# ScalarE computes the exact square of the hidden chunk in 26 slots, and adds the small term to the softmax sums

## The chip, the cores and the metric

The kernel runs on one core of a Trainium2 chip. The core has a matrix engine (TensorE, in the profile PE, with its weight loads as PEld), a vector engine (VectorE, DVE), an activation engine (ScalarE, ACT), a general engine (GpSimd, POOL) and a queue engine that issues most transfers (SyncE, SP). Each engine runs its own instruction list in order; semaphores hold an instruction until what it needs is done. The metric is the device time in microseconds of one execution, lower is better.

## The reference

Windowed attention, then a dense feed-forward layer with a squared ReLU, then eight experts of which each token uses one.

```python
scores = scale * np.matmul(q, k.transpose(0, 1, 3, 2))      # 4 x 8 heads, 576 positions, 64 wide
mask = (rel >= 0) & (rel < window)                          # window = 64
attn = np.exp(scores - np.max(scores, axis=-1, keepdims=True))
attn = attn / (np.sum(attn, axis=-1, keepdims=True) + 1e-09)
x = attn @ v                                                # 2304 tokens x 512
...
h = np.maximum(x @ w_in, 0.0)                               # w_in 512 x 2048
x = h * h @ w_out                                           # w_out 2048 x 512
...
expert_idx = np.argmax(x @ w_gate, axis=1)                  # 8 experts
out[mask] = gate_w[mask, None] * (np.maximum(xe @ w1[e], 0.0) @ w2[e])
```

## The kernel before

**Split numbers.** Products keep nearly full precision by splitting each operand into a rounded high part and a low part (the rest). `mm3` (lines 171 to 174) then makes three products: high by high, high by low, low by high.

**The dense layer in chunk slots.** Tokens go in 9 super-tiles of 256 (`st`), the 2048 hidden columns in 16 chunks of 128 (`f`). A slot is one pair (st, f): `gemm1` makes the chunk's 128 x 256 hidden values in a PSUM bank `h` (12 matmuls of 256 columns), `hidden` takes the ReLU into `r` on ScalarE (L462), `square` and `square_low` make the square as a high part `gh` and a low part `gl`, and two slots later `gemm2` adds the chunk to the output banks `y` (6 matmuls of 512 columns). There are two `h` banks, so `gemm1` of a slot waits until `gl` of the slot two before has been made. Slots 0 to 31 take super-tiles 0 and 1 in turns; the other 112 follow one super-tile after the other.

**The square before.** ScalarE squares `r` and rounds it in one instruction (L469, `gh`). VectorE makes the exact square `max(h, 0) * r` from the bank and `r` and writes it to the other half of the bank (L471), and then subtracts `gh` from it (L478, `gl`).

**Weight conversion.** In the first part of the dense layer the weights arrive as 64-bit numbers and are turned into fp32 on the chip, 16 conversions (0 to 15), one for each chunk f: a transfer to a staging tile, an absolute value on ScalarE (`conv_a`, L189), four VectorE instructions on 128 x 1024 words (`conv_b`, L205, L206, L207, L210), then two roundings on ScalarE and two subtractions (`conv_c`, L226 and L228) that stand mostly on GpSimd, every sixth on VectorE. Staging and work tiles (`stg`, `tmp`) hold two conversions; the transfer for conversion f + 2 is issued when conversion f's last VectorE instruction is done.

**Attention beside it.** For each of 36 groups: scores on TensorE, for later groups a mask and a maximum on VectorE (L383, L387), four exponentials with row sums on ScalarE, then `att_norm`: VectorE adds 1e-9 to the sums (L410) and inverts them (L411), GpSimd multiplies (L412). GpSimd also lays out the queries (L334).

**Order.** The code names the slot at which each piece is written, but up to the last dense super-tile the final order on each engine is chosen by a scheduler at build time; the expert part after that is written out by hand.

Of the kernel before, what the change touches and what calls it, by code (L numbers as in the profile page):

```python
# [16 lines left out]
ACTF = mybir.ActivationFunctionType  # L17
ALU = mybir.AluOpType
# [31 lines left out]
def kernel(  # L50
# [13 lines left out]
    nc = tc.nc  # L64
# [6 lines left out]
    NF = DFF // P  # L71
    ST = 256
# [50 lines left out]
    for half in range(2):  # L123
# [5 lines left out]
            out=mid, in_=mid, pattern=[[-1, P]], compare_op=ALU.is_ge, fill=NEG, base=W, channel_multiplier=1  # L129
# [260 lines left out]
    def att_exp(g):  # L390
        s, nmax = probs[g]
        tot = br.tile([P, HP], F32, "tot", 3)
        if g < NE:
            ps, s = s, sfirst[g % 4]
            for hp in range(HP):
                nc.scalar.activation(
                    s[:, hp, :], ps[:, hp * P:(hp + 1) * P], ACTF.Exp, bias=nmax[:, hp:hp + 1], scale=SCALE,
                    accum_out=tot[:, hp:hp + 1],
                )
            probs[g] = s, tot  # L400
            return
        for hp in range(HP):
            nc.scalar.activation(
                s[:, hp, :], s[:, hp, :], ACTF.Exp, bias=nmax[:, hp:hp + 1], accum_out=tot[:, hp:hp + 1]
            )
        probs[g] = s, tot

    def att_norm(g):
        s, tot = probs[g]
        nc.vector.tensor_scalar_add(tot, tot, 1.0e-9)  # L410
        nc.vector.reciprocal(tot, tot)  # L411
        nc.gpsimd.tensor_tensor(s, s, tot.unsqueeze(2).to_broadcast([P, HP, P]), op=ALU.mult)  # L412

# [51 lines left out]
    def square(st, f):  # L465
        ps, r = gT[st, f]
        gh = br.tile([P, ST], F32R, "gh", 3)
        gl = br.tile([P, ST], F32R, "gl", 3)
        nc.scalar.square(gh, r)  # L469

        nc.vector.scalar_tensor_tensor(  # L471
            out=ps[:, ST:2 * ST], in0=ps[:, :ST], scalar=0.0, in1=r, op0=ALU.max, op1=ALU.mult
        )
        gT[st, f] = ps, gh, gl

    def square_low(st, f):
# [403 lines left out]
    slot = {c: i for i, c in enumerate(order)}  # L880
# [12 lines left out]
    def chain(i, stages, x, gaps, most=2):  # L893
# [8 lines left out]
        return i  # L902

    ATT = (att_scores, att_max, att_exp, att_norm, att_transpose, att_evac, att_values, att_out)
    at(16, load_gates, 0)

# [18 lines left out]
    for g in range(2 * QB, NS * QB):  # L925
        st, j = divmod(g, QB)
# [19 lines left out]
    for i in range(-PRE, len(order) + LA):  # L946
        run(i, False)
        if 0 <= i - 1 < len(order):
            square(*order[i - 1])
            square_low(*order[i - 1])  # L950
        if 0 <= i < len(order):
            gemm1(*order[i])
        if i >= LA:
            st, f = order[i - LA]
            gemm2(st, f)
            if f == NF - 1:
                x2_out(st)
        run(i, True)
        if 0 <= i < len(order):
            hidden(*order[i])  # L960
# [194 lines left out]
```

## Time and profile before

| | |
|---|---|
| median of 3 runs | 835.53 us (834.1 to 836.63) |
| profiled execution | 832.06 us, of which its span 829.9 us |
| TensorE busy | 787.3 us, 95% of the span |
| VectorE busy | 530.4 us, 64% |
| ScalarE busy | 398.8 us, 48% |
| GpSimd busy | 269.9 us, 33% |
| mean granted TensorE clock | 0.987 |

The span runs from the first to the last instruction. Shares are means over stages with different limits: the conversion lies between about 10 and 131 us, the dense layer between about 34 and 522 us, the experts after it.

### The profile page before, as it was taken

How to read it: one execution, taken by the hardware profiler on the slowest of the kernel's cores; microseconds unless marked ns; L12 is line 12 of the kernel's file. 1: busy time of each engine (PE TensorE's matmuls, PEld its weight loads, DVE VectorE, ACT ScalarE, POOL GpSimd, SP SyncE). 2: the span in 40 equal slices, each digit the busy share in tenths (PEclk: the TensorE clock that was granted, in tenths of full speed). 3: DMA queues.
4: the chain of work that ended last, by engine and by line, in shares of the span. 5: the costliest groups of instructions: out<-in, count | busy, mean ns of one | idle time of the engine just before them, and what ended most of it. 6: DMA issues, size and time to landing. Idle time of an engine off the chain costs nothing.

```text
span 829.9 us, 14957 instructions
## 1 busy us (share of the span) xinstructions
PE 787.3 (95%) x5212; PEld 685.5 (83%) x5212; DVE 530.4 (64%) x1198; ACT 398.8 (48%) x1051; POOL 269.9 (33%) x262
## 2 busy tenths in 40 slices
PE   6889989999999999999999999989999999999894
PEld 5777878888888888888888897877898888888783
DVE  5799995984855947639467396568678654434110
ACT  6986663434444443534344345447577553434211
POOL 4646751112121221312211016165567541420201
PEclk9989999999999999999999999999999999999998
DMA  9845553111111111102020037366678644420101
GB/s 264 274 134 190 194 172 102 64 34 32 58 45 64 39 42 62 52 29 75 26 64 18 22 102 229 104 216 208 193 244 246 212 155 131 135 80 2 51 2 43
DMA packets 50860, 91.50 MB, mean 110 GB/s; under 512 B 8220, under 2 KB 24604, under 8 KB 50752
## 3 DMA queue, kind: packets, MB, share of 16 engines
q1 hardware_dynamic: 44688, 80.43, 30.3%
q0 software_dynamic: 6064, 9.63, 3.5%
q8 instruction: 69, 1.13, 0.6%
q14 instruction: 39, 0.32, 0.1%
HBM read 84.59 MB, written 13.81 MB: 119 GB/s over the span
## 4 chain that ended last, share of the span: by engine, by line
PE 66%; issue 13%; DVE 9%; DMA 5%; ACT 4%; POOL 1%; ACTq 0%; SPq 0%; POOLq 0%; DVEq 0%
PE h L172 11%; PE h L173 10%; PE h L174 10%; PE y L172 10%; PE y L174 9%; PE y L173 9%; PE a L360 2%; DMA stg<-in_moe_w_out 2%; PE a L433 2%; PE a L418 1%; DVE tmp L205 1%; DVE tmp L210 1%; PE a L683 1%; DVE tmp L207 1%; DMA out<-s,tab 1%
## 5 line engine op out<-in xcount | busy, mean ns | idle before, releaser
L172 PE MATMUL h<-xh,w 128*128 128x256 f32 (+3 forms) x864 | 262.9, 304 | 10.9 <-DVE gl L478 5.4
L174 PE MATMUL h<-xh,w 128*128 128x256 f32 (+3 forms) x864 | 255.6, 296 | 1.2 <-POOL w L228 1.2
L173 PE MATMUL h<-xl,w 128*128 128x256 f32 (+3 forms) x864 | 255.6, 296 | 0.9 <-DVE xl L169 0.5
L172 PEld LDWEIGHTS h<-xh,w 128*128 128x128 f32 x864 | 164.9, 191 | 27.6 <-DVE gl L478 9.6
L173 PEld LDWEIGHTS h<-xl,w 128*128 128x128 f32 x864 | 165.0, 191 | 9.1 <-DVE xl L169 0.9
L174 PEld LDWEIGHTS h<-xh,w 128*128 128x128 f32 x864 | 165.0, 191 | 4.3 <-POOL w L228 1.5
L462 ACT ACTIVATE r<-h 128x256 f32<-128x256 f32 x144 | 55.1, 382 | 203.7 <-PE h L174 197.9
L172 PE MATMUL y<-w,gh 128*128 128x512 f32 x294 | 119.2, 405 | 0.7 <-ACT gh L469 0.7
L770 DVE SCALAR_TENSOR_TENSOR ggl<-h,ggh 128x512 fp32r<-128x512 f32 (+1 forms) x69 | 46.2, 670 | 111.6 <-ACT ggh L769 111.5
L173 PE MATMUL y<-w,gh 128*128 128x512 f32 x294 | 116.4, 396 | 0.0
L471 DVE SCALAR_TENSOR_TENSOR h<-h,r 128x256 f32<-128x256 f32 x144 | 61.4, 426 | 84.0 <-ACT r L462 84.0
L174 PE MATMUL y<-w,gl 128*128 128x512 f32 x294 | 102.1, 395 | 0.5 <-DVE gl L770 0.5
L769 ACT ACTIVATE ggh<-h 128x512 fp32r<-128x512 f32 (+1 forms) x69 | 40.2, 583 | 125.5 <-PE h L174 96.2
L548 DVE SCALAR_TENSOR_TENSOR tmp<-tmp,stg 128x512 f32<-128x512 f32 x128 | 96.0, 750 | 0.8
L334 POOL COPY q<-qd 64x256 f32<-64x256 f32 x46 | 34.4, 749 | 143.9 <-PE a L360 142.5
L172 PE MATMUL y<-w,ggh 128*128 128x512 f32 x170 | 70.7, 416 | 0.0
L174 PE MATMUL y<-w,ggl 128*128 128x512 f32 x170 | 67.6, 398 | 1.7 <-DVE junk L996 1.1
L173 PE MATMUL y<-w,ggh 128*128 128x512 f32 x170 | 67.1, 395 | 0.0
L276 POOL TENSOR_TENSOR w<-stg,w 128x512 fp32r<-128x512 f32 x27 | 36.5, 1357 | 90.6 <-ACT w L275 87.6
L478 DVE TENSOR_TENSOR gl<-h,gh 128x256 fp32r<-128x256 f32 x144 | 60.5, 420 | 8.3 <-ACT gh L469 1.5
L172 PEld LDWEIGHTS y<-w,gh 128*128 128x128 f32 x294 | 55.6, 189 | 10.8 <-ACT gh L469 1.4
L173 PEld LDWEIGHTS y<-w,gh 128*128 128x128 f32 x294 | 55.6, 189 | 9.4
(165 smaller groups left out, 1262.4 us busy)
## 6 DMA issues: line engine op xcount, KB each, us to landing
stg<-in_moe_w SPq DMA_DIRECT2D x45, 512.0 KB, 4.0
stgx<-in_moe_w SPq DMA_DIRECT2D x18, 512.0 KB, 4.2
stg<-in_moe_w_in SPq DMA_DIRECT2D x16, 512.0 KB, 4.0
stg<-in_moe_w_out SPq DMA_DIRECT2D x16, 512.0 KB, 4.9
v<-in_v SPq DMA_DIRECT2D x28, 256.0 KB, 2.7
x_d<-tmp SPq DMA_DIRECT2D x18, 256.0 KB, 2.0
q<-in_moe_w SPq DMA_DIRECT2D x9, 512.0 KB, 4.5
qd<-in_q SPq DMA_DIRECT2D x28, 128.0 KB, 2.1
```

Of the source, the lines that this page charges most:

```text
L172: nc.tensor.matmul(o, lhsT=ah, rhs=bh, start=first, stop=False)
L173: nc.tensor.matmul(o, lhsT=ah, rhs=bl, start=False, stop=False)
L174: nc.tensor.matmul(o, lhsT=al, rhs=bh, start=False, stop=last)
L276: rest.tensor_tensor(l[:, a:a + 512], src, h[:, a:a + 512].bitcast(F32), op=ALU.subtract)
L334: nc.gpsimd.tensor_copy(qk[g][rows, :, half, :], d[rows])
L360: nc.tensor.matmul(ps[:, hp * P:(hp + 1) * P], lhsT=qt[:, :, hp] if g < NE else qt[:, hp], rhs=kt[:, :, hp, :], start=g >= NE, stop=g >= N ...
L462: nc.scalar.activation(r, gT[st, f][:, :ST], ACTF.Relu)
L471: nc.vector.scalar_tensor_tensor(out=ps[:, ST:2 * ST], in0=ps[:, :ST], scalar=0.0, in1=r, op0=ALU.max, op1=ALU.mult)
L478: nc.vector.tensor_tensor(gl, ps[:, ST:2 * ST], gh.bitcast(F32), op=ALU.subtract)
L548: nc.vector.scalar_tensor_tensor(out=junk, in0=x2sb[tt], scalar=1.0, in1=w, op0=ALU.mult, op1=ALU.mult, accum_out=l[:, t, e:e + 1])
L769: nc.scalar.activation(h[:, :width], hid[f][:, :width], ACTF.Relu)
L770: nc.vector.scalar_tensor_tensor(out=l[:, :width], in0=hid[f][:, :width], scalar=0.0, in1=h[:, :width].bitcast(F32), op0=ALU.max, op1=ALU. ...
```

## The change

ScalarE makes the exact square in the slots below 26 (2 x 16 - 6): it squares `r` into the free half of the bank and then copies it, rounded, to `gh`. From slot 26 on the square is made as before. In `att_norm` the addition of 1e-9 goes from VectorE to ScalarE, for all 36 groups.

```diff
@@ att_exp (both places where the exponentials end)
+        nc.scalar.activation(tot, tot, ACTF.Copy, bias=1.0e-9)
         probs[g] = s, tot
 
     def att_norm(g):
         s, tot = probs[g]
-        nc.vector.tensor_scalar_add(tot, tot, 1.0e-9)
         nc.vector.reciprocal(tot, tot)
@@ square
-        nc.scalar.square(gh, r)
-
-        nc.vector.scalar_tensor_tensor(
-            out=ps[:, ST:2 * ST], in0=ps[:, :ST], scalar=0.0, in1=r, op0=ALU.max, op1=ALU.mult
-        )
+        if slot[st, f] < 2 * NF - 6:
+            nc.scalar.square(ps[:, ST:2 * ST], r)
+            nc.scalar.copy(gh, ps[:, ST:2 * ST])
+        else:
+            nc.scalar.square(gh, r)
+            nc.vector.scalar_tensor_tensor(
+                out=ps[:, ST:2 * ST], in0=ps[:, :ST], scalar=0.0, in1=r, op0=ALU.max, op1=ALU.mult
+            )
```

Lines shift by 1 to 6: L471 stands in L477 after the change, L478 in L484, L411 in L412; the new ScalarE instructions are L473 (square), L474 (copy), L400 and L407 (addition). The scheduler then chooses another order in the first 32 slots.

VectorE before, at its 17th to 21st `gl` (slots 16 to 20): conversion 13 on `tmp_77`, conversion 14 on `tmp_76`, the first step of conversion 15 on `tmp_77`.

```order
162 L478 TENSOR_TENSOR gl_85<-h_435,gh_82 128x256
163 L207 SCALAR_TENSOR_TENSOR tmp_77<-stg_79,tmp_77 128x1024
164 L471 SCALAR_TENSOR_TENSOR h_434<-h_434,r_460 128x256
165 L210 SCALAR_TENSOR_TENSOR tmp_77<-stg_79,tmp_77 128x1024
166 L478 TENSOR_TENSOR gl_83<-h_434,gh_80 128x256
167 L205 TENSOR_SCALAR tmp_76<-tmp_76 128x1024
168 L471 SCALAR_TENSOR_TENSOR h_435<-h_435,r_461 128x256
169 L206 TENSOR_SCALAR tmp_76<-tmp_76 128x1024
170 L478 TENSOR_TENSOR gl_84<-h_435,gh_81 128x256
171 L207 SCALAR_TENSOR_TENSOR tmp_76<-stg_78,tmp_76 128x1024
172 L471 SCALAR_TENSOR_TENSOR h_434<-h_434,r_460 128x256
173 L210 SCALAR_TENSOR_TENSOR tmp_76<-stg_78,tmp_76 128x1024
```

Row 166 is the `gl` of slot 18: conversion 13 has just ended, and 14 and 15 stand behind it.

VectorE after the change, at its 17th to 20th `gl` (slots 16 to 19), with the same names for the conversions:

```order
131 L205 TENSOR_SCALAR tmp_76<-tmp_76 128x1024
132 L484 TENSOR_TENSOR gl_84<-h_435,gh_81 128x256
133 L206 TENSOR_SCALAR tmp_76<-tmp_76 128x1024
134 L207 SCALAR_TENSOR_TENSOR tmp_76<-stg_78,tmp_76 128x1024
135 L484 TENSOR_TENSOR gl_85<-h_436,gh_82 128x256
136 L210 SCALAR_TENSOR_TENSOR tmp_76<-stg_78,tmp_76 128x1024
137 L205 TENSOR_SCALAR tmp_77<-tmp_77 128x1024
138 L206 TENSOR_SCALAR tmp_77<-tmp_77 128x1024
139 L228 TENSOR_TENSOR w_658<-tmp_76,w_656 128x512
140 L207 SCALAR_TENSOR_TENSOR tmp_77<-stg_79,tmp_77 128x1024
141 L484 TENSOR_TENSOR gl_83<-h_435,gh_80 128x256
142 L210 SCALAR_TENSOR_TENSOR tmp_77<-stg_79,tmp_77 128x1024
```

Row 141 is the `gl` of slot 18: all of conversion 14, and conversion 15 but for its last instruction, now stand ahead of it.

ScalarE before, around the absolute value for conversion 14 (`tmp_76`):

```order
132 L462 ACTIVATE r_460<-h_434 128x256
133 L469 ACTIVATE gh_80<-r_460 128x256
134 L189 ACTIVATE tmp_76<-stg_78 128x1024
135 L462 ACTIVATE r_461<-h_435 128x256
136 L226 CAST w_655<-tmp_77 128x4x128
137 L226 CAST w_656<-tmp_77 128x512
138 L469 ACTIVATE gh_81<-r_461 128x256
```

ScalarE after the change, at the same place:

```order
163 L474 CAST gh_80<-h_436 128x256
164 L473 ACTIVATE h_435<-r_461 128x256
165 L189 ACTIVATE tmp_76<-stg_78 128x1024
166 L474 CAST gh_81<-h_435 128x256
167 L226 CAST w_655<-tmp_77 128x4x128
168 L226 CAST w_656<-tmp_77 128x512
169 L463 ACTIVATE r_462<-h_436 128x256
```

The absolute value, which waits for a transfer, now stands between the square and the rounding of one slot.

## Rows read from the trace of the kernel before

**Rows 1.** Busy time by stretch: stretch, its length, then PE, PEld, DVE, ACT, POOL.

```profile
80.00:118.00 38.00, 35.70 (x257) 29.72 (x255) 37.58 (x57) 25.44 (x66) 23.30 (x16) 1.00 0.55 187
118.00:131.00 13.00, 11.91 (x72) 9.99 (x72) 13.00 (x19) 6.53 (x14) 4.34 (x3) 1.00 0.48 161
131.00:161.00 30.00, 30.00 (x197) 27.24 (x197) 20.01 (x56) 11.78 (x35) 5.16 (x5) 1.00 0.19 66
```

**Rows 2.** VectorE by shape, 39.4 to 117.8 us: count, busy us, mean ns, idle before.

```profile
L207 DVE SCALAR_TENSOR_TENSOR tmp<-stg,tmp 128x1024 int32<-128x1024 int32 x11 | 16.7, 1515 | 0.0
L210 DVE SCALAR_TENSOR_TENSOR tmp<-stg,tmp 128x1024 int32<-128x1024 int32 x11 | 15.0, 1361 | 0.0
L206 DVE TENSOR_SCALAR tmp<-tmp 128x1024 int32<-128x1024 int32 x11 | 11.3, 1027 | 0.0
L205 DVE TENSOR_SCALAR tmp<-tmp 128x1024 f32<-128x1024 f32 x11 | 10.5, 959 | 0.8 <-ACT tmp L189 0.8
L471 DVE SCALAR_TENSOR_TENSOR h<-h,r 128x256 f32<-128x256 f32 x18 | 7.6, 420 | 0.2 <-ACT r L462 0.2
...
L383 DVE SCALAR_TENSOR_TENSOR s<-a,mask 128x512 f32<-128x512 f32 x6 | 4.1, 679 | 0.0
...
L228 DVE TENSOR_TENSOR w<-tmp,w 128x512 fp32r<-128x512 f32 x3 | 4.0, 1326 | 0.0
```

**Rows 3.** VectorE in order of time: start us, duration us, line, operation.

```profile
71.12 0.67 DVE L206 TENSOR_SCALAR tmp<-tmp 128x1024 int32<-128x1024 int32 x1
...
127.02 0.68 DVE L228 TENSOR_TENSOR w<-tmp,w 128x512 fp32r<-128x512 f32 x1
...
127.96 1.21 DVE L207 SCALAR_TENSOR_TENSOR tmp<-stg,tmp 128x1024 int32<-128x1024 int32 x1
129.09 0.42 DVE L471 SCALAR_TENSOR_TENSOR h<-h,r 128x256 f32<-128x256 f32 x1
```

**Rows 4.** VectorE in order of time, from the remainder of slot 18 on.

```profile
117.81 0.41 DVE L478 TENSOR_TENSOR gl<-h,gh 128x256 fp32r<-128x256 f32 x1
118.15 0.68 DVE L205 TENSOR_SCALAR tmp<-tmp 128x1024 f32<-128x1024 f32 x1
118.75 0.42 DVE L471 SCALAR_TENSOR_TENSOR h<-h,r 128x256 f32<-128x256 f32 x1
119.08 1.45 DVE L206 TENSOR_SCALAR tmp<-tmp 128x1024 int32<-128x1024 int32 x1
120.44 0.41 DVE L478 TENSOR_TENSOR gl<-h,gh 128x256 fp32r<-128x256 f32 x1
120.78 1.98 DVE L207 SCALAR_TENSOR_TENSOR tmp<-stg,tmp 128x1024 int32<-128x1024 int32 x1
```

**Rows 5.** GpSimd in order of time, at the same place.

```profile
118.62 3.05 POOL L228 TENSOR_TENSOR w<-tmp,w 128x512 fp32r<-128x512 f32 x2 [3.28 <-ACT w L226]
```

**Rows 6.** GpSimd by shape, 39.4 to 117.8 us.

```profile
L228 POOL TENSOR_TENSOR w<-tmp,w 128x512 fp32r<-128x512 f32 x18 | 30.6, 1714 | 12.4 <-ACT w L226 12.3
L412 POOL TENSOR_TENSOR s<-s,tot 128x512 f32<-128x512 f32 x6 | 8.3, 1385 | 12.3 <-DVE tot L411 12.3
L334 POOL COPY q<-qd 64x256 f32<-64x256 f32 x6 | 7.4, 1229 | 5.3 <-PE a L360 5.1
```

**Rows 7.** GpSimd by shape, 140 to 480 us, after the conversion.

```profile
L334 POOL COPY q<-qd 64x256 f32<-64x256 f32 x40 | 27.1, 677 | 138.6 <-PE a L360 137.4
L412 POOL TENSOR_TENSOR s<-s,tot 128x512 f32<-128x512 f32 x22 | 22.8, 1038 | 85.0 <-ACT xh L168 48.6 <-DVE tot L411 30.3 <-DVE ixf L566 3.4
```

**Rows 8.** ScalarE by shape: 39.4 to 117.8 us, the last row 0 to 140 us.

```profile
L189 ACT ACTIVATE tmp<-stg 128x1024 f32<-128x1024 f32 x11 | 12.7, 1155 | 11.0 <-DMA stg<-in_moe_w_out 7.4 <-POOL w L228 1.9 <-DVE tmp L207 1.5
...
L469 ACT ACTIVATE gh<-r 128x256 fp32r<-128x256 f32 x19 | 7.9, 416 | 0.4
...
L378 ACT ACTIVATE nmax<-nmax 128x4 f32<-128x4 f32 x8 | 1.7, 215 | 1.6 <-DVE nmax L375 1.6
```

**Rows 9.** ScalarE in order of time, the absolute value for conversion 15.

```profile
123.21 1.20 ACT L189 ACTIVATE tmp<-stg 128x1024 f32<-128x1024 f32 x1 [2.38 <-DMA stg<-in_moe_w_out]
```

More of the change, by code (lines that the diff above doesn't have):

```diff
@@ L405, in att_exp @@
             )
+        nc.scalar.activation(tot, tot, ACTF.Copy, bias=1.0e-9)
         probs[g] = s, tot
```

## The prediction

> **What bounds the kernel now.** The page's shares come first: TensorE 95%, VectorE 64%. Next come the stretches, since a share is a mean. From 131 us on TensorE is busy 30.00 of 30.00 us and VectorE only 20.01; before that it is the other way round, VectorE 37.58 of 38 and 13.00 of 13, TensorE 35.70 and 11.91 [rows 1]. So while weights are converted VectorE sets the pace, and afterwards TensorE does. The change can only move the moment at which TensorE's full stretch begins. Then comes VectorE by shape and in order of time. Its conversion steps take longer than they need: L206 0.67 us when nothing disturbs it, 1.03 in the mean; L207 1.21 against 1.52 [rows 2, 3]. In order of time L206 takes 1.45 and L207 1.98 just when GpSimd runs two L228 [rows 4, 5], while L471 and L478 beside them keep 0.42 and 0.41. So VectorE and GpSimd hinder each other, but not in the instructions with an operand in PSUM, which the change removes.
>
> By the Trainium skill (SBUF — State Buffer, section "SBUF: two separate sides"), GpSimd and VectorE instructions with two SBUF inputs or in a two-port mode exclude each other for a whole instruction. The rows agree in sign: L207 has two SBUF inputs and is stretched, L471 has one and is not.
>
> **Where I measure.** I compare the time of one instruction, the `gl` of slot 18, at 117.81 us before [rows 4]. By then both orders have had the same chunks and the same six masked groups on VectorE. The starting point is the first step of conversion 3, at 39.4 us, where the stretch of rows 2 begins. VectorE is in order, so what stands between the two is a sum.
>
> **Removed and added up to there.** An instruction costs the distance to the next start: L471 0.33 (118.75 to 119.08), L478 0.34, L205 0.60 [rows 4]; L207 1.13 (127.96 to 129.09); others their undisturbed duration less the same 0.08: L206, L228 and the attention's L383 0.60, L210 like L207 [rows 2, 3]. Removed: 18 L471 of 0.33, 5.9, and six additions of some 0.08, 0.5, in all 6.4 us. But the new order puts conversion 14 and most of 15 ahead of this `gl`; counted in the two lists: two L205 and two L206 more (2.4), two L207 (2.3), one L210 (1.1), two L228 on VectorE (1.2), one L169 (0.3), in all 7.3 us. Net **+0.9 us**: the relief is spent on conversions done earlier, which no slot needs yet (chunk 15 is first used in slot 26).
>
> **Waits on GpSimd.** Over the 11 conversions of rows 2 the stretching is 11 x 0.30 for L207, 11 x 0.15 for L210, 11 x 0.36 for L206, 11 x 0.28 for L205, 3 x 0.65 for L228: 14.0 us. GpSimd's own work up to there is 24 two-input instructions and six copies [rows 6]; undisturbed, L412 takes 1.04 and L334 0.68 [rows 7], and L228 has L412's form: 29.0 us. So 15.0 us of it were hidden, behind VectorE instructions that are not stretched. Of those there were 23.0 us: 18 L471, 19 L478, 7 L169, 12 of attention at 0.60 and the small ones. After the change there are 16.9 us, for 31.1 us of GpSimd (its order has two more L228 by then). With the old share hidden (65%) the waits are 20.1 us, +6.1; with all 16.9 used they are 14.2, +0.2. Where a single unstretched instruction stands between two conversion steps, as at 120.44, the next step waits 0.77 of a 1.04 us GpSimd instruction [rows 4]: 0.27 of 0.34 is used, 80%. I take that: 13.5 hidden, 17.6 of waits, **+3.6 us**.
>
> **What is given back.** After this `gl` the old order still has conversions 14 and 15, and TensorE idles 13.00 - 11.91 = 1.1 us by 131 us [rows 1]. The new one has one VectorE step left there, so I let all of this go: **-1.1 us**. Later slots run at TensorE's pace in both, and nothing is won or lost in them; the 22 later additions cost ScalarE some 0.2 us each under TensorE's work (ScalarE is busy 11.78 of 30 us there [rows 1]).
>
> **ScalarE.** Each slot gets one more instruction. The price of a square into PSUM no row shows; the nearest is L469's 0.42, and L469 is the same square [rows 8]. For 19 slots that is 8 us, and six additions like L378's 0.22 are 1.3. ScalarE was busy 25.44 of 38 us [rows 1], so there is room; the longer chain to `gl` (one instruction) lies behind the conversion step that stands ahead of `gl` on VectorE. If that cover were gone, each slot would pay up to 0.4. Before 39.4 us ScalarE is the busy engine; eight additions there cost 1 to 2 us, against casts and copies that the new order puts behind the absolute value for conversion 3. I cost it at nothing, within 1 us either way.
>
> The Trainium skill (ScalarE: Activation LUTs, section "Rules for kernel authors") tells to keep add and multiply on VectorE. Its cost for an activation with immediate bias gives 0.19 us for 4 elements, as an estimate, near L378; by it the early additions would cost 1.5 us, inside the bound above. No row here shows that addition on ScalarE.
>
> **Sum.** +0.9 + 3.6 - 1.1 = +3.4 us on the profiled 832.06, so 835.5. The median of the runs lies 3.5 us above that execution, so the forecast is **838.9 us**, slower by 0.4%. With the bounds of the waits (+0.2 to +6.1) and of the start (1 us) it goes from -1.0 to +6.9, that is 834.5 to 842.4. A measurement of this kernel can tell about 0.3%, 2.5 us, from no change: faster is below 833.0, slower above 838.0.
>
> **Rivals.**
> *No change to be measured.* Waits use nearly all that is left to hide behind, or the start comes 1 us sooner: the sum is between -1 and +2.4, 834.5 to 838. For it: the rows at 118 to 121 already show little waste. Against it: in the mean only 65% was used.
> *Faster.* GpSimd's instructions lose instead: with fewer VectorE instructions between, the next step has been issued before GpSimd asks, and GpSimd waits. It has time: 23.30 busy of 38 [rows 1], stretched as that is (L228 1.71 against 1.04 [rows 6, 7]). The sum turns measurably negative once the waits fall below 11.7 us; with a third fewer than before, 9.3, it is 0.9 - 4.7 - 1.1 = -4.9: 830.6 us. Against it: at 120.78 both asked, and VectorE waited. A conversion also needs its transfer: five of 11 absolute values waited for it, 7.4 us together [rows 8], and the one for conversion 15 ended at 124.41 [rows 9], 6.6 us after conversion 13, whose staging tile it needed, had ended just ahead of 117.81 [rows 4]; conversions that follow faster would wait there.
> *Slower through ScalarE.* In the new order the absolute value stands ahead of a slot's rounding. When it waits for its transfer, 2.38 us at 123.2 [rows 9], the rounding waits, then `gl`, and behind it on VectorE the conversion steps, whose end issues the next transfer. If half of the 13 waited 1 us more than now, this adds some 6 us: 845.
> *Half the change is inert.* The late additions do nothing under any rival.
>
> **Chances.** Forecast, slower by the waits, 0.30, its own range 838 to 842.4; slower through ScalarE 0.10; no change 0.35; faster 0.25. So faster 0.25, same 0.35, slower 0.40. The range that leaves out about 2 in 10 reaches into the faster case and to the upper bound: 831 to 843.5.
>
> **What would show it.** Right: `gl` of slot 18 at 120 to 122 us; conversion 15 ending one instruction behind it; VectorE fully busy until then and mean durations of L206 and L207 up from 1.03 and 1.52; TensorE's full stretch starting later. Wrong: that `gl` before 116, with L206 and L207 no longer than now. For the ScalarE rival: VectorE idle ahead of `gl` with ScalarE's rounding as releaser, and longer waits of L189 for transfers. The forecast fails if the two engines settle their conflict to GpSimd's cost, or if the order before 39.4 us brings the first slots more than 1 us sooner.

## The result, and the profile after

The changed kernel takes 842.71 us in the median (842.26 to 843.27), the kernel before 835.83 in the runs beside it (834.1 to 836.63): ratio 1.0100, 95% interval 1.0079 to 1.0122, slower by 6.9 us. The forecast had the sign and too small a size: 838.9, that is 3.1 us above those runs; the range to 843.5 holds the result. The profiled execution took 842.9 us, its span 841.2.

Busy time by stretch, after, columns as in [rows 1], then the granted TensorE clock, the share of the transfer engines and GB/s; below it the first 170 us before:

```profile
0.00:170.00 170.00, 144.69 (x1016) 124.10 (x1016) 132.81 (x206) 115.57 (x333) 78.38 (x75) 0.97 0.52 169
80.00:118.00 38.00, 31.91 (x238) 26.85 (x238) 37.57 (x45) 28.06 (x78) 25.39 (x19) 1.00 0.55 181
118.00:131.00 13.00, 11.87 (x73) 9.79 (x73) 11.10 (x12) 7.50 (x17) 5.83 (x5) 1.00 0.54 175
131.00:161.00 30.00, 30.00 (x195) 27.24 (x194) 13.15 (x36) 12.77 (x39) 2.94 (x4) 1.00 0.16 53
```

```profile
0.00:170.00 170.00, 150.82 (x1068) 129.79 (x1069) 144.64 (x274) 109.60 (x301) 76.65 (x75) 0.98 0.53 172
```

VectorE is as full as before up to 118 us, with 45 instructions where there were 57. TensorE has lost 3.8 us in the same stretch. From 131 us on TensorE is full again: nothing is lost there. Over the first 170 us TensorE's busy time is 144.69 us after and 150.82 before, 6.1 us less. The granted clock of this stretch, 0.97 against 0.98, can account for some 1.5 us of 145 (an estimate from these two rows).

The two profiled spans differ by more than the medians do: 841.2 and 829.9, 11.3 us. The end of the dense layer tells how much of that is the change; the first rounding behind its last slot stands here, before and after:

```profile
522.45 0.59 ACT L168 CAST xh<-a 128x512 fp32r<-128x512 f32 x1 [0.20 <-PE a L683]
529.08 0.59 ACT L168 CAST xh<-a 128x512 fp32r<-128x512 f32 x1
```

That is 6.6 us, near the 6.9 of the medians. The other 4.7 us lie in the experts, which took from 307 to 312 us in the traces of both kernels and of e1 to e15, without regard to what a run lost (308.7 in the slowest, e13). So the loss has arisen by the end of the dense layer, most of it in the first 170 us.

VectorE after, by shape, from the first step of conversion 3 (38.24 us) to the `gl` of slot 18 (127.29), to be read against [rows 2]:

```profile
L207 DVE SCALAR_TENSOR_TENSOR tmp<-stg,tmp 128x1024 int32<-128x1024 int32 x13 | 22.7, 1748 | 0.2
L210 DVE SCALAR_TENSOR_TENSOR tmp<-stg,tmp 128x1024 int32<-128x1024 int32 x12 | 16.6, 1381 | 0.1
L206 DVE TENSOR_SCALAR tmp<-tmp 128x1024 int32<-128x1024 int32 x13 | 15.9, 1223 | 0.2
L205 DVE TENSOR_SCALAR tmp<-tmp 128x1024 f32<-128x1024 f32 x13 | 10.8, 830 | 3.3 <-ACT tmp L189 3.1
L484 DVE TENSOR_TENSOR gl<-h,gh 128x256 fp32r<-128x256 f32 x18 | 7.3, 407 | 0.0
...
L228 DVE TENSOR_TENSOR w<-tmp,w 128x512 fp32r<-128x512 f32 x5 | 6.9, 1374 | 0.2 <-ACT w L226 0.2
```

L207 went from 1515 to 1748 ns, L206 from 1027 to 1223, while L205 became shorter (959 to 830); `gl`, with one operand in PSUM, stayed at 407 (410 before). So in the mean the disturbance by GpSimd grew where it already was. By the rule of the Trainium skill that the prediction cites (SBUF — State Buffer, section "SBUF: two separate sides") a VectorE instruction with at most one SBUF input, outside the two-port modes, doesn't contend with GpSimd. The rows of L207 and `gl` agree; L206 has one SBUF input, so it agrees only if it runs in a two-port mode, which no row here names.

VectorE after in order of time, first the step that opens this stretch, then the `gl` of slot 18 and the last step of conversion 15:

```profile
38.24 1.24 DVE L205 TENSOR_SCALAR tmp<-tmp 128x1024 f32<-128x1024 f32 x1 [1.12 <-ACT tmp L189]
...
127.29 0.41 DVE L484 TENSOR_TENSOR gl<-h,gh 128x256 fp32r<-128x256 f32 x1
127.62 1.21 DVE L210 SCALAR_TENSOR_TENSOR tmp<-stg,tmp 128x1024 int32<-128x1024 int32 x1
```

The `gl` is 9.5 us later than before (117.81 in [rows 4]), and conversion 15 ends one instruction behind it. GpSimd and ScalarE after, same stretch, to be read against [rows 6] and [rows 8]:

```profile
L228 POOL TENSOR_TENSOR w<-tmp,w 128x512 fp32r<-128x512 f32 x21 | 35.7, 1718 | 22.8 <-ACT w L226 22.7
L413 POOL TENSOR_TENSOR s<-s,tot 128x512 f32<-128x512 f32 x6 | 7.8, 1305 | 11.4 <-DVE tot L412 11.4
L334 POOL COPY q<-qd 64x256 f32<-64x256 f32 x6 | 7.3, 1211 | 1.9 <-PE a L360 1.7
L413 POOL TENSOR_TENSOR sf<-sf,tot 128x512 f32<-128x512 f32 x1 | 1.0, 1037 | 0.0
```

```profile
L189 ACT ACTIVATE tmp<-stg 128x1024 f32<-128x1024 f32 x12 | 13.9, 1157 | 15.4 <-DMA stg<-in_moe_w_out 13.4 <-POOL w L228 2.0
L474 ACT CAST gh<-h 128x256 fp32r<-128x256 f32 x20 | 7.4, 371 | 0.3
L473 ACT ACTIVATE h<-r 128x256 f32<-128x256 f32 x19 | 7.4, 389 | 0.2
...
L407 ACT ACTIVATE tot<-tot 128x4 f32<-128x4 f32 x6 | 1.2, 203 | 0.1
```

The absolute value now waits 13.4 us for its transfers (7.4 before). What TensorE waits for between 40 and 120 us, after (us in total, times, longest):

```profile
PE y L172 <- ACT gh L474: 6.6, 6, 2.8
PE h L172 <- DVE gl L484: 4.2, 5, 1.6
PE a L360 <- DVE tot L412: 2.4, 1, 2.4
```

Before, the same view of the same stretch:

```profile
PE h L172 <- DVE gl L478: 2.9, 5, 1.1
PE a L418 <- DVE s L383: 1.5, 1, 1.5
...
PE y L172 <- ACT gh L469: 0.5, 1, 0.5
```

The wait for `gl`, on which the prediction argued, grew by 1.3 us. The wait of the second layer's product (`gemm2`, which reads `gh`) for the rounding grew by 6.1, and the prediction has no term for it; nor has it one for the 2.4 us of one wait for softmax sums (`tot`). The longest wait for `gh`, after, ScalarE ahead of it and TensorE:

```profile
39.37 0.43 ACT L473 ACTIVATE h<-r 128x256 f32<-128x256 f32 x1
39.69 1.31 ACT L332 COPY q<-qd 64x256 f32<-64x256 f32 x2
41.03 0.37 ACT L474 CAST gh<-h 128x256 fp32r<-128x256 f32 x1
```

```profile
41.45 0.50 PE L172 MATMUL y<-w,gh 128*128 128x512 f32 x1 [2.81 <-ACT gh L474]
```

ScalarE is busy all the while; two copies of queries stand between the square and its rounding. Of the six waits only two, 0.41 and 0.30 us, follow closely on an absolute value that waited for its transfer.

### The profile page after: what moved, and what is told of

Same layout as the page of the kernel before. It is cut to its first block, busy times and chain, and to the rows that moved or that the text cites. A ratio compares the mean times of both kernels' runs of the same rounds, so it can differ in the third digit from the quotient of the medians.

```text
span 841.2 us, 14933 instructions
## 1 busy us (share of the span) xinstructions
PE 790.6 (94%) x5212; PEld 687.8 (82%) x5212; DVE 520.4 (62%) x1136; ACT 409.1 (49%) x1113; POOL 272.1 (32%) x262
## 4 chain that ended last, share of the span: by engine, by line
PE 68%; issue 13%; DVE 8%; ACT 5%; DMA 4%; POOL 1%; SPq 0%; POOLq 0%; ACTq 0%; DVEq 0%
PE h L172 11%; PE h L173 10%; PE h L174 10%; PE y L172 10%; PE y L174 10%; PE y L173 9%; DMA stg<-in_moe_w_out 3%; PE a L360 2%; PE a L434 2%; PE a L419 1%; DVE tmp L207 1%; DVE w L276 1%; DVE tmp L210 1%; PE a L689 1%; ACT tmp L189 1%
## 5 line engine op out<-in xcount | busy, mean ns | idle before, releaser
L477 DVE SCALAR_TENSOR_TENSOR h<-h,r 128x256 f32<-128x256 f32 x118 | 50.6, 429 | 79.3 <-ACT r L463 79.2
L554 DVE SCALAR_TENSOR_TENSOR tmp<-tmp,stg 128x512 f32<-128x512 f32 x128 | 94.0, 735 | 0.8
L484 DVE TENSOR_TENSOR gl<-h,gh 128x256 fp32r<-128x256 f32 x144 | 60.5, 420 | 34.7 <-ACT gh L476 15.2
L172 PEld LDWEIGHTS y<-w,gh 128*128 128x128 f32 x294 | 55.5, 189 | 19.1 <-ACT gh L474 10.0
L413 POOL TENSOR_TENSOR s<-s,tot 128x512 f32<-128x512 f32 x28 | 31.9, 1138 | 102.0 <-DVE tot L412 85.1
```

What stands on the lines that cost most here:

```text
L172: nc.tensor.matmul(o, lhsT=ah, rhs=bh, start=first, stop=False)
L477: nc.vector.scalar_tensor_tensor(out=ps[:, ST:2 * ST], in0=ps[:, :ST], scalar=0.0, in1=r, op0=ALU.max, op1=ALU.mult)
L484: nc.vector.tensor_tensor(gl, ps[:, ST:2 * ST], gh.bitcast(F32), op=ALU.subtract)
L554: nc.vector.scalar_tensor_tensor(out=junk, in0=x2sb[tt], scalar=1.0, in1=w, op0=ALU.mult, op1=ALU.mult, accum_out=l[:, t, e:e + 1])
```

## Experiments

Medians of the kernel before, run beside them, were 833.13 (e1 to e4), 833.73 (e5 to e8), 832.91 (e9 to e12) and 833.35 us (e13 to e15). The microseconds in the expectations of e1 to e4 were reckoned from the 835.8 of the result, 2.7 above the before of these runs: there the ratio is the measure.

### First: conversions held, the chain, and each half of the change alone

**e1, conversions held.** Each conversion's first VectorE step is issued behind the `gl` behind which it stood before; the conversions are also written at later slots for it, and the rows of the gate are loaded at slot 24 instead of 16.

```diff
+    HOLD = {4: 1, 5: 3, 6: 4, 7: 6, 8: 7, 9: 10, 10: 11, 11: 13, 12: 15, 13: 17, 14: 19, 15: 21}
+        if f in HOLD:
+            hold.enter_context(tc.issue_after(done["gl", HOLD[f] - 1].ins))
```

> The changed kernel, with each conversion's first VectorE step held behind the gl of the slot behind which it stood before the change (conversions 13, 14 and 15 behind the 17th, 19th and 21st gl instead of the 15th, 16th and 18th); the gate rows are loaded later for it. Order theory (the loss comes from conversions standing ahead of slots that do not need them): most of the 6.9 us comes back, 834 to 838. Port theory (the loss comes from the longer stretching of VectorE's steps by GpSimd, wherever they stand): a third comes back, about 840. ScalarE theory (the rounding behind the absolute value and behind the square): nothing comes back, 841 to 844.

Measured: 839.29 us, ratio 1.0060 (1.0041 to 1.0078).

**e2, no chain on ScalarE.** The rounding comes first and both are made from `r`.

```diff
-            nc.scalar.square(ps[:, ST:2 * ST], r)
-            nc.scalar.copy(gh, ps[:, ST:2 * ST])
+            nc.scalar.square(gh, r)
+            nc.scalar.square(ps[:, ST:2 * ST], r)
```

> The changed kernel, but the rounded part comes straight from r as before and the exact square after it, so that the two ScalarE instructions do not wait for one another; as many instructions on ScalarE as in the change, the rounded part ready one instruction sooner. The scheduler puts the conversions nearly where they stood before (15 behind the 20th gl). ScalarE theory and order theory both: back to 834 to 838, the first by shorter waits of TensorE for gh (7.5 us with the change), the second by the places of the conversions. Port theory: still 840 to 843, as the products are gone from VectorE here too.

Measured: 836.78 us, ratio 1.0037 (1.0020 to 1.0053). TensorE's waits for `gh` between 40 and 120 us are 3.6 us, against 6.6 in the changed kernel.

**e3, the squares alone** (the addition stays on VectorE).

> Only the square goes to ScalarE; the small term stays on VectorE. The scheduler's order has conversion 15 behind the 20th gl, not the 18th. Order theory: 835 to 838. Port theory: 840 to 843, since all 26 products are gone. ScalarE theory: 841 to 843, the chain is the same.

Measured: 834.60 us, ratio 1.0008 (0.9992 to 1.0023): no change. So taking the products off VectorE costs nothing here, where the port theory and the ScalarE theory both wanted the whole loss; the `gl` of slot 18 stands at 117.73 us, as before.

**e4, the addition alone** (the squares stay on VectorE).

> Only the small term goes to ScalarE; the square stays as before. All three theories: within 2 us of the kernel before (834 to 838); a larger loss would mean that the additions in the softmax at the start are what costs.

Measured: 839.09 us, ratio 1.0062 (1.0041 to 1.0084). All my theories had the addition at next to nothing, and it carries most of the loss; e1, which puts only the conversions back, keeps more than half of it. So the theories fell. In e4's trace the additions themselves are short. The longest of TensorE's waits between 40 and 100 us looks like this, first ScalarE, then TensorE, in order of time:

```profile
50.47 1.15 ACT L189 ACTIVATE tmp<-stg 128x1024 f32<-128x1024 f32 x1 [2.24 <-DMA stg<-in_moe_w_out]
51.52 0.39 ACT L404 ACTIVATE s<-s,nmax 128x128 f32<-128x128 f32 x1
...
51.91 0.36 ACT L463 ACTIVATE r<-h 128x256 f32<-128x256 f32 x1
...
53.32 0.41 ACT L476 ACTIVATE gh<-r 128x256 fp32r<-128x256 f32 x1
```

```profile
53.78 0.79 PE L172 MATMUL y<-w,gh 128*128 128x512 f32 x1 [3.63 <-ACT gh L476]
```

The absolute value stands ahead of a slot's ReLU and rounding and waits 2.24 us for its transfer; three exponentials stand between ReLU and rounding; TensorE idles 3.63 us. No addition is in this chain: what differs is the order in which ScalarE's old instructions stand. That gave theory B (the loss is the order that the scheduler draws up anew once VectorE's list has changed) against theory A (the moved addition itself).

### Second: the addition in pieces

**e5, added on both engines.**

```diff
     def att_norm(g):
         s, tot = probs[g]
+        nc.vector.tensor_scalar_add(tot, tot, 1.0e-9)
         nc.vector.reciprocal(tot, tot)
```

(on e4, so ScalarE adds too)

> The kernel before, with the small term added on ScalarE and once more on VectorE where it stood (the sums come out 1e-9 larger). VectorE's list keeps its addition, so the order that the scheduler draws up stays nearer to that of before (an early stretch of VectorE reads almost the same), while ScalarE carries all 36 additions of the changed kernel. Theory A, the additions cost by standing in ScalarE's line and in the chain from the sums to the normalisation: as slow as the addition alone, ratio 1.005 to 1.008 (837.5 to 840 us against 833). Theory B, the loss comes from the order in which the engines' lists are drawn up once VectorE's addition is gone: within 2.5 us of before, ratio 0.997 to 1.003.

Measured: 839.33 us, ratio 1.0063 (1.0035 to 1.0092). Theory A had this right; theory B had 0.997 to 1.003 and missed.

**e6, added nowhere** (e4 without its two `nc.scalar.activation(tot, tot, ...)` lines).

> The kernel before with the small term left out altogether (no addition on any engine). Theory A: nothing stands on ScalarE and VectorE is 36 x 0.15 us lighter, so not slower than before, ratio 0.995 to 1.001. Theory B: VectorE's list has lost the same 36 instructions as with the addition on ScalarE, so the lists are drawn anew, and the time may come out some microseconds off on either side; 1.002 to 1.008 would speak for B, and no other theory gives it.

Measured: 836.88 us, ratio 1.0032 (1.0011 to 1.0054). With 36 instructions fewer and none moved it is slower than before. Theory A has no room for that.

**e7 and e8, the first 8 groups and the 28 later ones alone** (a condition `g < NE` or `g >= NE` on e4's lines).

> The kernel before, with the small term added on ScalarE for the first 8 attention groups only (those before the dense part starts); the 28 later groups add it on VectorE. Theory A, in the form that the start is where ScalarE is full (9.95 us of 10 between 30 and 40): all of the loss, ratio 1.004 to 1.008. Theory A in the form that later additions hold up the normalisations: within 1 us of before. Theory B: the conversions stand one slot further apart than with all additions moved, as in before from slot 19 on, so half the loss or less, ratio 0.999 to 1.004.

> The kernel before, with the small term added on ScalarE for the 28 later attention groups only; the first 8 add it on VectorE. Theory A, start: within 1 us of before, ratio 0.999 to 1.001. Theory A, later normalisations: all of the loss, ratio 1.004 to 1.008. Theory B: the order of the start is that of before, the later order is new; ratio 0.999 to 1.005, and this run's loss and that of the run with the first 8 need not add up to the loss of all 36.

Measured: e7 834.92 us, ratio 1.0018 (1.0001 to 1.0035); e8 835.24 us, ratio 1.0023 (1.0005 to 1.0041). Together 0.4%, where the whole is 0.6%; the intervals are too wide to say that the two don't add up. Each form of theory A wanted all of the loss, 1.004 to 1.008, in one of the two, and neither run comes to it. e5 would still fit theory A, so the order had to be tested by itself.

### Third: the order by itself

In these kernels each engine's instructions up to the experts are held in the order in which they stand in another kernel. `PLACES` has, for each engine, the places of the instructions as the code writes them, in the order wanted; an edge orders an instruction behind the one ahead of it on its own engine and waits for nothing.

```diff
+PLACES = {
+    'Pool': [
...
+    for engine, places in PLACES.items():
+        row = [pinned[engine][p] for p in places]
+        for a, b in zip(row, row[1:]):
+            tc.add_manual_dep(
+                b, a.name, mybir.DependencyInfo(mybir.DependencyClass.NoSync, mybir.DependencyReason.DATA), reason="order"
+            )
```

**e9, the changed kernel in the order of before.**

> The changed kernel, with each engine's instructions of everything up to the experts held in the order in which they stand in the kernel before (an ordering edge from each to the next on its engine, no wait): the 36 additions stand on ScalarE right behind the last exponential of their group, each rounding of the 26 right behind its exact square, and TensorE, GpSimd and the transfers stand as before. Theory B (the loss is the order that the scheduler drew up anew, not the moved work): all of the loss is gone, ratio 0.990 to 1.002. Theory A (the moved work itself: the longer chain and ScalarE's line): the loss stays, ratio 1.005 to 1.010. Half and half, since the addition left out altogether cost 3 us and the addition on both engines 5.6: 1.002 to 1.005.

Measured: 834.20 us, ratio 1.0012 (0.9995 to 1.0030): the loss is gone. The lines of its code are moved by the table (L474 is L207, L477 L210, L473 L206, L472 L205, L495 L228, L741 the rounding). VectorE by shape from conversion 3 (38.9 us) to the `gl` of slot 18, now at 117.26:

```profile
L474 DVE SCALAR_TENSOR_TENSOR tmp<-stg,tmp 128x1024 int32<-128x1024 int32 x11 | 16.7, 1520 | 0.1
L477 DVE SCALAR_TENSOR_TENSOR tmp<-stg,tmp 128x1024 int32<-128x1024 int32 x11 | 14.7, 1333 | 0.1
L473 DVE TENSOR_SCALAR tmp<-tmp 128x1024 int32<-128x1024 int32 x11 | 11.9, 1078 | 0.2
L472 DVE TENSOR_SCALAR tmp<-tmp 128x1024 f32<-128x1024 f32 x11 | 10.2, 927 | 2.5 <-ACT tmp L456 2.5
...
L495 DVE TENSOR_TENSOR w<-tmp,w 128x512 fp32r<-128x512 f32 x4 | 5.7, 1420 | 0.8 <-ACT w L493 0.8
```

These are nearly the durations of [rows 2] (1515, 1361, 1027, 959), although 18 products fewer lie between. The traced execution was the slowest of the twelve (837.88 us); the end of its dense layer is 1.3 us later than before. Busy time by stretch and TensorE's waits between 40 and 120 us, e9:

```profile
80.00:118.00 38.00, 36.41 (x261) 30.50 (x261) 35.20 (x43) 30.50 (x80) 23.76 (x16) 1.00 0.52 181
```

```profile
PE y L439 <- ACT gh L741: 4.8, 3, 3.0
PE h L439 <- DVE gl L751: 1.4, 2, 1.0
```

VectorE is no longer full (35.20 of 38, 37.58 before): the time taken off it stands as idle time, and TensorE waits for the rounding.

**e10, the addition alone in the order of before.**

> Only the addition moved to ScalarE (squares as in the kernel before), in the order of the kernel before, each addition right behind the last exponential of its group. Theory B: ratio 0.997 to 1.002. Theory A: as the addition alone, 1.005 to 1.008.

Measured: 832.66 us, ratio 0.9990 (0.9974 to 1.0006). 36 additions on ScalarE, in the chain from the sums to the normalisation, cost nothing that these runs can tell. Nor do the ordering edges, unless the two offset each other.

**e11, the kernel before in the order of the changed one.**

> The kernel before, not an instruction added or left out, in the order of the changed kernel: TensorE, GpSimd and the transfers stand as in the changed kernel, each square on VectorE right ahead of the subtraction that reads it, each addition right ahead of its reciprocal. Theory B: slow with nothing moved, ratio 1.005 to 1.012 (VectorE's list is 26 products longer in an order drawn up without them). Theory A: ratio 0.997 to 1.003.

Measured: 849.07 us, ratio 1.0194 (1.0167 to 1.0221). The expectation had 1.005 to 1.012: the sign was right, the size beyond it. VectorE by shape from conversion 3 (39.1 us) to the `gl` of slot 18 at 135.67 (lines as in e9, but `gl` L745 and the rounding L736), TensorE's waits between 40 and 120 us, and the first 170 us by engine:

```profile
L474 DVE SCALAR_TENSOR_TENSOR tmp<-stg,tmp 128x1024 int32<-128x1024 int32 x13 | 22.0, 1691 | 0.2
L477 DVE SCALAR_TENSOR_TENSOR tmp<-stg,tmp 128x1024 int32<-128x1024 int32 x12 | 15.5, 1294 | 0.1
L473 DVE TENSOR_SCALAR tmp<-tmp 128x1024 int32<-128x1024 int32 x13 | 14.9, 1148 | 0.2
L472 DVE TENSOR_SCALAR tmp<-tmp 128x1024 f32<-128x1024 f32 x13 | 11.4, 879 | 0.0
...
L495 DVE TENSOR_TENSOR w<-tmp,w 128x512 fp32r<-128x512 f32 x5 | 6.3, 1251 | 0.6 <-ACT w L493 0.6
```

```profile
PE h L439 <- DVE gl L745: 9.7, 8, 2.2
PE y L439 <- ACT gh L736: 2.6, 2, 1.4
```

```profile
0.00:170.00 170.00, 137.17 (x956) 118.16 (x957) 137.02 (x221) 103.97 (x284) 73.85 (x75) 0.97 0.52 167
```

The 13 conversions of the changed kernel are back, and most of the lengthening of L207 (1691 ns, after 1748) and L206 (1148, after 1223), with not one instruction changed. The order of the changed kernel has no places for VectorE's products and additions; each was put right ahead of its reader, a choice that may cost by itself.

**e12, the kernel before in the order of e5.**

> The kernel before, not an instruction added or left out, in the order of the kernel that adds the small term on both engines (5.6 us slower than before, ratio 1.0063), its additions on ScalarE left out. Theory B: as slow as that kernel, ratio 1.004 to 1.008. Theory A: ratio 0.997 to 1.002.

Measured: 839.43 us, ratio 1.0079 (1.0050 to 1.0107), as slow as e5 (1.0063), without a single addition on ScalarE. In its trace the `gl` of slot 18 is only 0.2 us later than before (118.03) and the end of the dense layer 3.1 us; where the rest of the 6.5 us arises isn't shown. The granted clock of the first 170 us was 0.95 in e12 and 0.96 in e5 (0.98 before): how much of these two losses is clock isn't separated here.

### Fourth: which engine's order

**e13 and e14, the changed kernel with TensorE's order of before alone, and with VectorE's and GpSimd's alone** (`PLACES` with these engines only). The scheduler still draws up the lists that aren't held, and it draws them anew: in conversion 3 the changed kernel's VectorE does L206, L228, L169 and then L207 (39.52 to 42.01 us), while in e13 L207 comes right behind L206, ahead of L228 and L169 (40.12 to 44.39). So neither run is the changed kernel with one list exchanged.

> The changed kernel with TensorE's instructions alone held in the order of the kernel before; the other engines stay the scheduler's. If TensorE's order (where slots and attention groups stand) carries the loss: ratio 0.998 to 1.003. If VectorE's and GpSimd's order (conversions ahead of slots, GpSimd's subtractions beside VectorE's long instructions) carries it: 1.005 to 1.010. In between, the loss is in how they stand to each other.

> The changed kernel with VectorE's and GpSimd's instructions held in the order of the kernel before; TensorE, ScalarE and the transfers stay the scheduler's. If VectorE's and GpSimd's order carries the loss: ratio 0.998 to 1.003, and VectorE's time beyond its fastest durations falls from 23.7 us (to the subtraction of slot 18) to about the 17 of before. If TensorE's carries it: 1.005 to 1.010.

Measured: e13 854.57 us, ratio 1.0268 (1.0235 to 1.0301); e14 840.97 us, ratio 1.0098 (1.0077 to 1.0119). Neither brings the loss back to nothing, and TensorE's order alone makes it worse than either whole order: its wait for the rounding between 40 and 120 us is then

```profile
PE y L349 <- ACT gh L651: 8.8, 6, 4.4
```

Part of that loss is clock: the granted clock of the first 170 us was 0.90 in e13, 0.98 before, and 8% of its 137.71 busy us is some 11 us of the 21, an estimate from these figures. In e14 VectorE's steps up to the `gl` of slot 18 (126.08 us) wait less for GpSimd: by the prediction's sum 16.4 us for 11 conversions (from 18.5, 15.3, 12.0 and 9.9 us for L207, L210, L206 and L205 and 4.9 for four L228), against 21.7 for 13 after and 14.0 for 11 before (worked out below). The loss is all there even so, and VectorE idles for ScalarE's rounding instead:

```profile
L535 DVE TENSOR_TENSOR gl<-h,gh 128x256 fp32r<-128x256 f32 x19 | 7.8, 410 | 5.3 <-ACT gh L525 5.3
```

So restoring TensorE's list, or VectorE's and GpSimd's, doesn't repair the loss, and that it lies in how the lists stand to each other is the reading that is left, not one that is shown. ScalarE's list alone, the obvious suspect by this row, and that of the transfers were not tested.

**e15, e2 in the order of before.**

> The changed kernel in the order of the kernel before, with ScalarE's two instructions both made from r, the rounded square first and the exact one behind it, so that TensorE finds the rounding as early as in the kernel before. If the kept order gained nothing (ratio 1.0012) because TensorE waits for the rounding (4.8 us of such waits between 40 and 120, 0.5 in the kernel before): 2 to 4 us less than that run, ratio 0.993 to 0.999. If the conversions' own chain (loads, ScalarE's absolute value) sets the end and VectorE only idles for it: within 1.5 us of that run, ratio 0.999 to 1.003.

Measured: 833.83 us, ratio 1.0002 (0.9986 to 1.0017). TensorE's wait for the rounding fell from 4.8 to

```profile
PE y L439 <- ACT gh L740: 1.9, 1, 1.9
```

but the time by no more than 0.1%, inside both intervals. With the kept order the change is worth nothing that these runs can tell, with or without the chain, as the second expectation had it, and no version here beats the kernel before.

## Why the prediction was half right

**The bound** was right in the main: most of the loss arises while weights are converted, and from 131 us on TensorE is full in both. That VectorE alone sets the pace there was not: after, TensorE waits longer for ScalarE's `gh` (6.6 us) than for VectorE's `gl` (4.2).

**Removed and added** was right. From the rows after: two more of L205, L206, L207 and L228, one more L210, 18 fewer products: the +0.9 us of the two lists. The start came 1.2 us sooner (38.24 against 39.4), 0.2 more than I allowed.

**Waits on GpSimd** is the term of the sum that was mis-sized: +3.6, bounds +0.2 to +6.1. By the prediction's own undisturbed durations, taken off the busy times of the rows after (22.7 - 13 x 1.21, 16.6 - 12 x 1.21, 15.9 - 13 x 0.67, 10.8 - 13 x 0.68, 6.9 - 5 x 0.68), the waits are 21.7 us after, 14.0 before: **+7.7**, outside its bounds. GpSimd's work was larger than in my bound, 27 instructions of 1.04 and six of 0.68, 32.2 us instead of 31.1 (the `sf` row began ahead of the stretch). Of it 32.2 - 21.7 = 10.5 us were hidden, 62% of the 16.9 us available: near the mean share of before (65%), and I had put 80% in its place, read from one spot at 120.44 us.

The reason I gave for that term, that the products are gone behind which GpSimd worked, carries the smaller part. The same sum gives 18.9 us for e11, where all products are back in the new order, and 15.0 for e9, where they are gone in the old one. So their going is worth 1.0 us (e9 against before) to 2.8 (after against e11), and the new order by itself 4.9 (e11 against before). About half of that is the two conversions more that the new order has there, at 14.0 / 11 = 1.3 us each as before.

**Idle time of VectorE** was not in the sum: ahead of L205 it is 3.3 us, 1.1 of them ahead of the first, against 0.8 before: +1.4. Together -1.2 + 0.9 + 7.7 + 1.4 = 8.8 of the 9.5 us by which the `gl` of slot 18 is late (127.29 us, forecast 120 to 122); 0.7 stay unassigned.

**Given back** was, by the end of the dense layer, 9.5 - 6.6 = 2.9 us in the two profiled executions, not 1.1. That the time still lies in the range is in part luck: a term outside its bounds and one left out were met by more given back.

**ScalarE** at nothing is the other step that failed. It holds for the moved work in the old order (e10: 0.9990 for the additions, e9: 1.0012 for all of it). But I asked only whether `gl` waits for the longer chain. `gh` has a second reader, TensorE's second product, and its wait grew from 0.5 to 6.6 us. The rival "slower through ScalarE" had the engine right and longer waits of L189 for transfers (7.4 to 13.4 us), but the wrong one to suffer, VectorE instead of TensorE; and the absolute value stands close ahead of only two of the six waits, 0.7 of the 6.6 us. In the others query copies and exponentials stand there.

**The step behind all this** is that I took the new order as a list of which I priced two moved conversions, and let the rest stand as neutral. Runs e9 to e12 show that the order is the loss: the changed work in the old order 1.0012, the old work in the new order 1.0194. Up to 0.3% for the work itself can't be excluded (e9's interval ends at 1.0030). In the new order the moved squares and additions do help, by the step from 1.0194 to 1.0100, some 0.9%, as far as the places chosen for VectorE's products in e11 are fair; in the old order they help by nothing, and VectorE then idles. Which feature of the order costs the most stays open: holding the conversions (e1), TensorE's list (e13) or VectorE's and GpSimd's (e14) doesn't repair it. That the scheduler's picture lacks the waits between VectorE and GpSimd would fit, but no run tested it.

## What to carry to other kernels

Where a scheduler sets the order, a change in a list has two effects, the work moved and the order drawn up anew, and the second can be the larger: cost each by itself, by running the new work in the old order and the old work in the new. Price a new order by everything that reads the moved result, on every engine, and take a share of hidden time from the mean of the stretch, not from the one spot that looks tidy. A move that gains nothing in the old order needs a schedule made for it before it is judged.

## What the runs showed that I had not expected

- 36 instructions of 0.19 us in the mean left out and no other line touched (e6): slower by 0.3%, the order being drawn up anew.
- The same instructions in another valid order (e11): 16 us, 1.9% of the whole kernel; TensorE is busy 13.65 us less in the first 170 us (137.17 against 150.82).
- ScalarE's square from SBUF into PSUM took 389 ns and its rounding from PSUM 371, each less than the 416 ns of square and rounding in one, from SBUF to SBUF [rows 8]; the addition on 128 x 4 took 203.
